# Cross-attention on one core: each group's output store sent as two DMAs divided at a partition that changes from group to group

## The chip, the cores and the metric

The kernel runs on one core of a Trainium2 chip. The core has five engines with queues of their own: TensorE (PE, with weight loads listed as PEld), VectorE (DVE), ScalarE (ACT), GpSimd (POOL) and SyncE (SP), which here only issues DMAs. 16 DMA engines move data between device memory and the on-chip memory of 128 partitions. The metric is the device time of one execution in microseconds. The kernel before took 1207.94 us in the median of 3 runs (1204.18 to 1209.92).

## The reference, cut to what matters

```
B, H, Sq, Sk, D = 16, 32, 192, 1024, 128          # bf16 inputs q, k, v
scores = einsum("bhqd,bhkd->bhqk", q, k) * D ** -0.5
p = softmax(scores, axis=-1)
out = einsum("bhqk,bhkd->bhqd", p, v)
```

There are 512 heads, each with 192 rows of queries and 1024 keys. The output has 98,304 rows of 128 bf16 values, 256 bytes each.

## The kernel before, in words

The 512 heads are worked through in 32 groups of 16 (G=16, L34). Two heads form a pair with 384 query rows, which are three units of 128 rows: the first 128 rows of one head (A), the last 128 of the other (B), and one made of the 64 rows left over from each (S). A group has 8 pairs and 24 units.

Each unit passes through five steps: TensorE multiplies Q by K into PSUM (qk, L237 to L270); VectorE copies the scaled scores out and takes the row maximum (rowmax, L328 to L335); the exponential is taken by ScalarE directly (L373), or, for the units named in SHIFTED, GpSimd subtracts the maximum (L207) and ScalarE takes the exponential later (L384); TensorE transposes the result in 8 blocks (tr, L272 to L283) and ScalarE moves it out of PSUM (L384, L386); TensorE multiplies it by V (pv, L285 to L319). VectorE then normalises a pair with one multiplication into the tile ob (outputs, L347 to L362). The order of the steps on TensorE, VectorE and ScalarE is written out by hand in PE_ORDER, DVE_ORDER and ACT_ORDER (L17 to L20), with a period of six units.

All DMAs are issued by SyncE, in the order of its program (L136 to L193). K, Q and V have two buffers each (NS=2), the output tile ob has two as well (NSO=2, slot so = g % 2). For each group g SyncE does this:

- `loads(g + 2)` (L157 to L165): waits on s_qk until TensorE has done the last Q-K product of group g, which frees the buffers of K and Q; issues the transposing load of K (L141, 4 MB) and that of q (L145, 768 KB); waits on s_pv until group g's last product with V is done; issues the load of V (L152, 4 MB, 2 KB runs).
- `stores(g, ...)` (L167 to L174): waits on s_on until VectorE has written all 8 pairs of group g, and issues the store of 768 KB (L170). Its source is 128 partitions with 24 rows of 256 bytes each.

So the DMAs stand in the queue as K, q, V, store, K, q, V, store, one set for each group. The first group's loads are cut into three pieces (FIRST), the last group's store into four (LAST): 31 stores of 768 KB and one each of 384, 192, 96 and 96 KB, 35 in all.

A DMA adds 16 to its semaphore when it has landed, one for each of 16 completions. `store_cnt(g)` (L127) gives the count of sst at which group g's store is done; VectorE waits for it before the first pair of group g+2 overwrites the slot (L352, L353), and SyncE waits at the end for all stores (L189 to L193). TensorE waits for K and q of a group in qk (L256 to L268) and for V in pv (L306 to L313).

Of the kernel before, what the change touches and what calls it, by code (L numbers as in the profile page):

```python
# [31 lines left out]


def _attention_kernel(nc, q, k, v, out, G=16, NS=2, NSS=4, NX=4, NPT=5,  # L34
                      FIRST=((0, 2), (2, 8), (8, 16)), LAST=((0, 4), (4, 6), (6, 7), (7, 8))):
    B, H, SQ, D = q.shape
    SK = k.shape[2]
    assert D == 128 and SK == 1024 and SQ == 192, (D, SK, SQ)
# [9 lines left out]
    NSO = 2  # L48
# [5 lines left out]
    of = out.rearrange("b h s d -> (b h) s d")  # L54
# [15 lines left out]
    with ExitStack() as es:  # L70
        def sb(name, shape, dt):
            return es.enter_context(nc.sbuf_tensor(name, shape, dt))
# [4 lines left out]
        def sem(name):  # L77
            return es.enter_context(nc.semaphore(name))
# [4 lines left out]
        ob = sb("ob", [128, NSO, PPG, 3, 128], BF16)  # L83
# [14 lines left out]
        svl = [sem("svl%d" % i) for i in range(NS)]  # L98
        sf = [sem("sf%d" % i) for i in range(len(FIRST))]
        sfv = [sem("sfv%d" % i) for i in range(len(FIRST))]  # L100
        sst = [sem("sst%d" % i) for i in range(NSO)]
# [23 lines left out]
            return 16 * (g // NS + 1 - (g % NS == 0))  # L125

        def store_cnt(g):  # L127
            return 16 * (g // NSO + 1)

        def wait_x(eng, u):  # L130
            eng.wait_ge(s_xp if shifted(u) else s_xa, x_cnt[u])  # L131
# [4 lines left out]
        @block.sync  # L136
        def _(e):
            def load_kq(g, a, b, sems):
                s = g % NS
                h0 = g * G  # L140
                e.dma_start_transpose(  # L141
                    kt[:, s, :, a * 128:b * 128],
                    kf[h0 + a:h0 + b].rearrange("g (p t) d -> (g p) (t d)", t=KT_TILES),
                ).then_inc(sems[0], 16)
                e.dma_start_transpose(  # L145
                    qt[:, s, a * SQ:b * SQ],
                    qf[h0 + a:h0 + b].rearrange("g r d -> (g r) d"),
                ).then_inc(sems[1], 16)

            def load_v(g, a, b, sm):  # L150
                h0 = g * G
                e.dma_start(  # L152
                    vs[:, g % NS, a:b],
                    vf[h0 + a:h0 + b].rearrange("g (p t) d -> p g t d", t=KT_TILES),
                ).then_inc(sm, 16)

            def loads(g):  # L157
                s = g % NS
                last_u = (g - NS + 1) * UPG - 1
                if g >= NS:  # L160
                    e.wait_ge(s_qk, last_u + 1)
                load_kq(g, 0, G, (sxk[s], sxq[s]))
                if g >= NS:
                    e.wait_ge(s_pv, last_u + 1)
                load_v(g, 0, G, svl[s])  # L165

            def stores(g, a, b):  # L167
                so = g % NSO
                e.wait_ge(s_on, g * PPG + b)
                e.dma_start(  # L170
                    of[g * G + 2 * a:g * G + 2 * b].rearrange("h r d -> (h r) d").rearrange(
                        "(n p) d -> p n d", p=128),
                    ob[:, so, a:b].rearrange("p pg y d -> p (pg y) d"),
                ).then_inc(sst[so], 16)  # L174

            n = len(FIRST)
            for i in range(n):
                load_kq(0, *FIRST[i], (sf[i], sf[i]))
                if i > 0:
                    for i2 in range(i if i > 1 else 0, i + 1):  # L180
                        load_v(0, *FIRST[i2], sfv[i2])
            for g in range(1, min(NS, NGR)):
                loads(g)
            for g in range(NGR):
                if g + NS < NGR:
                    loads(g + NS)
                for a, b in (LAST if g == NGR - 1 else ((0, PPG),)):
                    stores(g, a, b)
            for so in range(min(NSO, NGR)):  # L189
                n_uses = len(range(so, NGR, NSO))  # L190
                if so == (NGR - 1) % NSO:
                    n_uses += len(LAST) - 1
                e.wait_ge(sst[so], 16 * n_uses)  # L193

        @block.gpsimd
        def _(gp):
# [20 lines left out]
        def _(pe):  # L217
# [19 lines left out]
            def qk(u):  # L237
# [13 lines left out]
                if g == 0:  # L251
                    for i, (h, _) in enumerate(FIRST):
                        if h <= b and i not in seen_kq:
                            seen_kq.add(i)
                            pe.wait_ge(sf[i], 32)
                elif u % UPG == 0:  # L256
                    pe.wait_ge(sxq[s], load_cnt(g))
# [27 lines left out]
            def pv(u):  # L285
# [14 lines left out]
                for t in range(KT_TILES):  # L300
                    first = t == 0
                    last = t == KT_TILES - 1
                    for at, rows, x in tiles:
                        w = PTS[:, t, rows]
                        pe.ldweights(w, tile_position=at)  # L305
                        if first and at[1] == 0:  # L306
                            if g == 0:
                                for i, (h, _) in enumerate(FIRST):
                                    if h <= b and i not in seen_v:
                                        seen_v.add(i)  # L310
                                        pe.wait_ge(sfv[i], 16)
                            elif u % UPG == 0:
                                pe.wait_ge(svl[s], load_cnt(g))  # L313
                            if k3 == 0 and pr >= 2:
                                pe.wait_ge(s_on, pr - 1)
                        ins = product(O[rows, sl, :], w, vs[:, s, x, t, :], at, first, last)
                        if with_rs:
                            ins = product(O[rows, 3, sl: sl + 1], w, ones[:, 0:1], at, False, last)
# [8 lines left out]
        def _(dve):  # L327
# [19 lines left out]
            def outputs(pr):  # L347
                g = pr // PPG
                pg = pr % PPG
                so = g % NSO  # L350
                dve.wait_ge(s_pv, max(pv_cnt[u] for u in pair_units(pr)))
                if pg == 0 and g >= NSO:  # L352
                    dve.wait_ge(sst[so], store_cnt(g - NSO))  # L353
                sel = slots_of(pr, True)
                dve.reciprocal(rinv[:, pr % 2, sel], o_ps[pr % 2][:, 3, sel]).then_inc(s_ri, 1)  # L355
                dve.wait_ge(s_ri, 2 * pr + 2)
                dve.tensor_tensor(  # L357
                    ob[:, so, pg],
                    o_ps[pr % 2][:, 0:3, :],
                    rinv[:, pr % 2, 0:3].unsqueeze(2).to_broadcast([128, 3, 128]),  # L360
                    ALU.mult,
                ).then_inc(s_on, 1)  # L362
# [30 lines left out]
def bass_standalone__mha_softmax__near_ridge_kernel(  # L393
    nc: bass.Bass,
    q: bass.AP,
    k: bass.AP,
    v: bass.AP,
    out: bass.AP,
):
    _attention_kernel(nc, q, k, v, out)  # L400
# [28 lines left out]
```

## Time and profile before

| | before |
|---|---|
| median of 3 runs | 1207.94 us (1204.18 to 1209.92) |
| profiled execution | 1203.52 us, of which the span is 1201.8 us |
| busy: PE, PEld, DVE, ACT, POOL | 94%, 70%, 91%, 90%, 40% |
| DMA | 321.34 MB, mean 267 GB/s; 789,893 packets, of them 724,176 under 512 B |
| issue to landing, median: K, q, V, store of 768 KB | 30.4, 6.1, 15.1, 17.1 us |
| chain that ended last | PE 51%, DMA 34%, SP's queue 14% of the span |
| DVE wait for PE s_ps, ACT wait for PE pt_ps (L386) | 77.1 us, 78.4 us |

The span is the time from the first to the last instruction of the profiled execution. A busy share is an average over the whole span. DMA rates of the profile count all 16 engines together, so that one engine that moves 256-byte packets alone shows as a small number in a window of short slices. In lists of instructions, "SPq" stands for SyncE's queue: its time is the time for which an issuing instruction was held, not the time of the transfer. A line such as "L220 PE MATMUL o_ps<-vs,pt_sb" names the helper `product`, which records every product; the tiles tell which step it is.

### The profile page before, as it was taken

The page shows a single profiled execution, that of the slowest core. Times are in us where ns is not written, and L with a number is a line of the kernel's source. Part 1 is how long each engine was busy: PE and PEld are TensorE (multiplying, and loading weights), DVE is VectorE, ACT ScalarE, POOL GpSimd, SP SyncE. Part 2 cuts the span into 40 slices and gives each one's busy share as a digit, 9 for nine tenths or more (in the row PEclk, how much of TensorE's full clock was granted, in tenths as well). Part 3 has the DMA queues.
Part 4 walks back from the last instruction along what each step waited for, and adds up shares of the span by engine and source line. Part 5 has one row for each costly group of instructions (what it writes and reads, how often), then busy time and mean ns, then how long its engine had stood idle before and what let it go on. Part 6 is the DMA issues. An engine that isn't in the chain of part 4 may idle for free.

```text
span 1201.8 us, 40191 instructions
## 1 busy us (share of the span) xinstructions
PE 1123.8 (94%) x18432; PEld 844.7 (70%) x15360; DVE 1089.6 (91%) x2304; ACT 1083.3 (90%) x1793; POOL 485.3 (40%) x262
## 2 busy tenths in 40 slices
PE   5599999999999999999999999999999899999998
PEld 3477777777677777776776777777776667777776
DVE  5589998999899999999998999999998899989897
ACT  4689998999899999999998999999998899989898
POOL 2234443444343443443434444343443344334343
PEclk9899999999999999999999999999999999999999
DMA  9999999999999999999999999999999999999991
GB/s 238 238 280 293 264 279 263 267 295 265 289 269 254 275 294 289 274 279 251 279 289 268 293 259 259 295 278 288 291 230 264 281 284 288 264 248 295 275 274 41
DMA packets 789893, 321.34 MB, mean 267 GB/s; under 512 B 724176, under 2 KB 724176, under 8 KB 789712
## 3 DMA queue, kind: packets, MB, share of 16 engines
q1 hardware_dynamic: 789712, 318.78, 111.9%
q8 instruction: 132, 2.16, 0.7%
q14 instruction: 49, 0.40, 0.1%
HBM read 134.22 MB, written 25.17 MB: 133 GB/s over the span
## 4 chain that ended last, share of the span: by engine, by line
PE 51%; DMA 34%; SPq 14%; issue 1%; ACT 1%; DVE 0%; DVEq 0%
DMA vs<-in_v_dram 34%; PE o_ps L220 18%; PE pt_ps L220 17%; PE s_ps L220 16%; SPq L145 8%; SPq L141 5%; ACT x_sb L373 0%; DVE ss L332 0%; SPq L152 0%; ACT pt_sb L384 0%; ACT pt_sb L386 0%; DVE ob L357 0%; DVE rinv L355 0%; DVEq L131 0%
## 5 line engine op out<-in xcount | busy, mean ns | idle before, releaser
L332 DVE TENSOR_SCALAR_CACHE_REDUCE ss<-s_ps 128x1024 f32<-128x1024 f32 x768 | 920.8, 1220 | 95.8 <-PE s_ps L220 77.1
L207 POOL TENSOR_TENSOR x_sb<-ss,nb 128x1024 bf16<-128x1024 f32 x256 | 484.6, 1893 | 704.5 <-DVE ss L332 689.0
L305 PEld LDWEIGHTS <-pt_sb 128*128 128x128 bf16 (+1 forms) x8192 | 442.0, 104 | 238.0 <-issue 140.4
L373 ACT ACTIVATE x_sb<-ss,nb 128x1024 bf16<-128x1024 f32 x512 | 585.4, 1145 | 12.7 <-DVE ss L332 12.7
L220 PE MATMUL o_ps<-vs,pt_sb 128*128 128x128 bf16 (+1 forms) x8192 | 495.9, 219 | 38.6 <-DMA vs<-in_v_dram 38.5
L220 PE MATMUL s_ps<-kt,qt 128*128 128x512 bf16 (+1 forms) x2048 | 466.2, 386 | 35.0 <-DMA qt<-in_q_dram 33.5
L220 PE MATMUL pt_ps<-ident,x_sb 128*128 128x128 bf16 x6144 | 451.3, 220 | 1.3 <-ACT pt_sb L384 1.3
L279 PEld LDWEIGHTS <-x_sb 128*128 128x128 bf16 x6144 | 366.2, 98 | 62.5 <-issue 62.1
L386 ACT ACTIVATE pt_sb<-pt_ps 128x512 f32<-128x512 f32 x512 | 306.0, 598 | 78.6 <-PE pt_ps L220 78.4
L384 ACT ACTIVATE pt_sb<-pt_ps 128x1024 bf16<-128x1024 bf16 x256 | 260.1, 1016 | 21.9 <-PE pt_ps L220 21.9
L220 PE MATMUL o_ps<-ones,pt_sb 128*128 128x1 bf16 x2048 | 189.3, 165 | 0.0
L357 DVE TENSOR_TENSOR ob<-o_ps,rinv 128x384 bf16<-128x384 f32 x256 | 142.7, 557 | 8.8
L263 PEld LDWEIGHTS <-qt 128*128 128x128 bf16 (+1 forms) x1024 | 79.3, 103 | 53.3 <-DMA qt<-in_q_dram 30.5
L373 ACT ACTIVATION_READ_ACCUMULATOR x_sb<-ss,nb 128x1 f32 x512 | 100.7, 197 | 0.0
L332 DVE DVE_READ_ACCUMULATOR ss<-s_ps 128x1 f32 x768 | 63.7, 83 | 0.0
L355 DVE RECIPROCAL rinv<-o_ps 128x1 f32<-128x1 f32 x256 | 41.7, 163 | 4.3 <-PE o_ps L220 4.3
L345 DVE RECIPROCAL rinv<-rs 128x2 f32<-128x2 f32 x256 | 40.9, 160 | 1.1 <-ACT x_sb L373 1.1
L373 ACT ACT_TABLE_LOAD x1 | 1.3, 1283 | 0.8 <-PEq L414 0.8
L199 POOL TENSOR_SCALAR_AFFINE_SELECT ident<-ones 128x128 bf16<-128x128 bf16 x1 | 0.3, 292 | 0.1
L197 POOL MEMSET ones<- 128x128 bf16 x1 | 0.2, 204 | 0.3 <-POOLq L414 0.3
L414 POOL MEMSET const-float32-0.0<- 128x1 f32 x1 | 0.1, 98 | 0.3 <-issue 0.3
L414 POOL MEMSET const-bfloat16-1.0<- 128x1 bf16 x1 | 0.1, 101 | 0.0
(2 smaller groups left out, 0.2 us busy)
## 6 DMA issues: line engine op xcount, KB each, us to landing
vs<-in_v_dram SPq DMA_DIRECT2D x31, 4096.0 KB, 15.1
out_dram<-ob SPq DMA_DIRECT2D x31, 768.0 KB, 17.1
vs<-in_v_dram SPq DMA_DIRECT2D x1, 2048.0 KB, 10.4
vs<-in_v_dram SPq DMA_DIRECT2D x1, 1536.0 KB, 8.4
kt<-in_k_dram SPq DMA_TRANSPOSE x34, 30.4
qt<-in_q_dram SPq DMA_TRANSPOSE x34, 6.1
vs<-in_v_dram SPq DMA_DIRECT2D x1, 512.0 KB, 4.4
out_dram<-ob SPq DMA_DIRECT2D x1, 384.0 KB, 3.2
```

The source lines that it names most:

```text
L141: e.dma_start_transpose(kt[:, s, :, a * 128:b * 128], kf[h0 + a:h0 + b].rearrange("g (p t) d -> (g p) (t d)", t=KT_TILES),).then_inc(sems[ ...
L145: e.dma_start_transpose(qt[:, s, a * SQ:b * SQ], qf[h0 + a:h0 + b].rearrange("g r d -> (g r) d"),).then_inc(sems[1], 16)
L207: gp.tensor_tensor(x_sb[:, u % NX, :], ss[:, u % NSS, :], nb[:, u % NSS: u % NSS + 1].to_broadcast([128, SK]), ALU.subtract,).then_inc(s_x ...
L220: return pe.add_instruction(mybir.InstMatmult(name=nc.get_next_instruction_name(), engine=mybir.EngineType.PE, ins=[pe.lower_ap(x), pe.low ...
L263: pe.ldweights(w, tile_position=at)
L279: pe.ldweights(w, is_transpose=True, tile_position=(0, 0))
L305: pe.ldweights(w, tile_position=at)
L332: dve.tensor_scalar(ss[:, u % NSS, :], s_ps[u % 2][:].rearrange("p t k -> p (t k)"), -scale, None, ALU.mult, ALU.min, accum_out=nb[:, u % ...
L357: dve.tensor_tensor(ob[:, so, pg], o_ps[pr % 2][:, 0:3, :], rinv[:, pr % 2, 0:3].unsqueeze(2).to_broadcast([128, 3, 128]), ALU.mult,).then ...
L373: act.activation(x_sb[:, u % NX, :], ss[:, u % NSS, :], ACT_FN.Exp, bias=nb[:, u % NSS: u % NSS + 1], scale=-1.0, accum_out=rs[:, pr % NRS ...
L384: act.activation(pt_sb[:, u % NPT], pt_ps[u % 2][:], ACT_FN.Exp, scale=-1.0).then_inc(s_ev, 1)
L386: act.activation(words(pt_sb[:, u % NPT]), words(pt_ps[u % 2][:]), ACT_FN.Copy).then_inc(s_ev, 1)
```

## The change

Each store is issued as two DMAs. The first carries partitions 0 to cut-1, the second the rest. The cut is 126 for group 0, 117 for group 1, 108 for group 2, 121 for group 3, and so on in turn. Both DMAs add 16 to the same semaphore, so the counts that are waited for are doubled. The four pieces of the last group (group 31) are each divided at 121. The order in SyncE's queue, all waits of the other engines and the bytes moved stay the same.

```diff
 def _attention_kernel(nc, q, k, v, out, G=16, NS=2, NSS=4, NX=4, NPT=5,
-                      FIRST=((0, 2), (2, 8), (8, 16)), LAST=((0, 4), (4, 6), (6, 7), (7, 8))):
+                      FIRST=((0, 2), (2, 8), (8, 16)), LAST=((0, 4), (4, 6), (6, 7), (7, 8)), STORE_CUTS=(126, 117, 108, 121)):
...
         def store_cnt(g):
-            return 16 * (g // NSO + 1)
+            return 32 * (g // NSO + 1)
...
             def stores(g, a, b):
                 so = g % NSO
                 e.wait_ge(s_on, g * PPG + b)
-                e.dma_start(
-                    of[g * G + 2 * a:g * G + 2 * b].rearrange("h r d -> (h r) d").rearrange(
-                        "(n p) d -> p n d", p=128),
-                    ob[:, so, a:b].rearrange("p pg y d -> p (pg y) d"),
-                ).then_inc(sst[so], 16)
+                rows = of[g * G + 2 * a:g * G + 2 * b].rearrange("h r d -> (h r) d").rearrange(
+                    "(n p) d -> p n d", p=128)
+                cut = STORE_CUTS[g % len(STORE_CUTS)]
+                for lo, hi in ((0, cut), (cut, 128)):
+                    e.dma_start(
+                        rows[lo:hi],
+                        ob[lo:hi, so, a:b].rearrange("p pg y d -> p (pg y) d"),
+                    ).then_inc(sst[so], 16)
...
-                e.wait_ge(sst[so], 16 * n_uses)
+                e.wait_ge(sst[so], 32 * n_uses)
```

## The prediction

> **What bounds the kernel now.** I read the page's busy rows first, then the waits, then the sync queue's timeline, then the DMA rates in short windows.
>
> ```profile
> PE 1123.8 (94%) x18432; PEld 844.7 (70%) x15360; DVE 1089.6 (91%) x2304; ACT 1083.3 (90%) x1793; POOL 485.3 (40%) x262
> ...
> DMA  9999999999999999999999999999999999999991
> ...
> L220 PE MATMUL o_ps<-vs,pt_sb 128*128 128x128 bf16 (+1 forms) x8192 | 495.9, 219 | 38.6 <-DMA vs<-in_v_dram 38.5
> ```
>
> TensorE, VectorE and ScalarE are each busy 90% or more, yet TensorE still waits 38.5 us for V, 27 times, about once in each group of 16 heads, and the DMA row is full to the end. So the pace comes from the DMA engines, with TensorE close behind. From 400 to 1000 us TensorE waits 24.3 us for V in some 16.5 groups, 1.5 us in each. A group takes 36.4 us from V's arrival to the next V's arrival (mean over the trace's 31 V completions), so with no wait TensorE could do it in about 34.9: no gain here can pass 1.5 us a group.
>
> The sync queue in one period:
>
> ```profile
> 493.63 0.58 SPq L152 DMA_DIRECT2D vs<-in_v_dram  x1
> 494.25 4.52 SPq L170 DMA_DIRECT2D out_dram<-ob  x1
> 498.82 26.36 SPq L141 DMA_TRANSPOSE kt<-in_k_dram  x1
> 525.22 4.49 SPq L145 DMA_TRANSPOSE qt<-in_q_dram  x1
> 529.75 0.58 SPq L152 DMA_DIRECT2D vs<-in_v_dram  x1
> ```
>
> The four kinds of DMA follow one another without a gap: V, store, K transpose, q transpose. The view of waits puts 790 us of L141 down to TensorE's s_qk, but K's packets are flowing during that "wait"; the instruction is held because the queue in front of it is full. What the engines do at the seam from store to K transpose, in slices of 0.2 us from 504 to 512:
>
> ```profile
> DMA  9999999999999999999999999997321238999999
> GB/s 369 389 399 369 399 379 369 399 348 389 399 389 392 320 311 369 276 283 274 278 279 283 284 288 289 287 254 174 85 49 36 64 92 200 238 172 247 283 292 291
> ```
>
> V runs at 370 to 400 GB/s until 507, the store at about 280 until 509.2. Then the rate falls to 36 GB/s: most of the 16 engines have finished their share, and two have not. The transposes reach their full 290 GB/s only at 511.4. The trace records 16 completions for each store; here 14 of them come from 509.52 to 510.24 and two at 511.33 and 511.36. Over the 29 stores in front of a K transpose, the 14th of 16 comes on the average 0.86 us after the first, the 15th 1.47 and the last 1.96. In the trace the full rate starts within 0.4 us of that last completion in nearly all of the 29. **So a store costs the path what its latest engine costs**; the others wait for it.
>
> Why do the transposes wait for one engine? A window inside a K transpose, 0.1 us a slice from 481 to 485, shows it:
>
> ```profile
> GB/s 292 289 294 287 287 289 443 274 269 271 205 20 18 3 0 0 0 3 8 8 10 10 8 10 10 118 289 289 287 294 297 289 287 287 289 289 294 289 289 289
> ```
>
> At 481.6 one 16 KB packet of queue q8 (TensorE's instruction fetch: 132 packets, 2.16 MB) goes in. All transposing stops for 1.5 us, during which a lone engine catches up at 8 to 10 GB/s, and then all go on. The transposes move in step, so one late engine stops all 16. The late engines of a store are likewise those that a fetch has hit during V or the store: fetches come every 8.8 us and take 1.04 us.
>
> **The change, part by part.** It alters only SP's list: 35 store DMAs become 70, and every other instruction keeps its place. No instruction of another engine moves; only their line numbers do.
>
> 1. *How the load is dealt.* Now 128 partitions x 24 rows of 256 B = 3072 packets, 192 for each of 16 engines, 8 partitions each. No DMA of this trace has another number of partitions than 128, so the dealing of 126 is my assumption: equal whole shares, on as many engines, at most 16, as divide the number, from the first engine on. Then 126+2 gives 14 engines 9 partitions and two of these one more; 117+11 gives 10 on eleven engines, 9 on two; 108+20 gives 11 on ten, 9 on two; 121+7 gives 12 on seven, 11 on four. Heaviest engine against 8 partitions: +48, +48, +72 and +96 packets. At 290 GB/s / 16 a packet takes 14.1 ns, so +0.68, +0.68, +1.02, +1.36 us. Two to five engines, the last in number, get nothing: 2.7 us less.
> [...]
>
> 2. *Which engines are late now.* This decides the sign. The one place where I can count them is the tail, where DMAs start on idle engines. The store of 192 KB around 1193.3, in slices of 0.1 us from 1193 to 1197:
>
> ```profile
> GB/s 0 0 0 54 230 243 220 218 210 212 210 359 108 8 0 0 0 0 0 0 0 3 8 8 10 8 10 10 3 0 0 0 0 0 0 0 0 0 0 0
> ```
>
> A fetch goes in at 1194.16, and one engine does the second half of its share alone, from 1195.1. In the three other stores of the tail the 16 engines end in a staggered order, about 11 ns apart with a step after the seventh. Laid on that order, the 15 undisturbed ends miss the last but one: shifted by 8 to 16 ns all others fit, and with any other place left out the fit is worse. If engines are started in the order of their numbers, the fetch sits on the 15th, which gets no store at all after the change. That is one fetch; that the second late engine is its neighbour is a guess. I take both as relieved.
>
> 3. *The sum.* With the two late engines empty, a store ends with its 14 others, 0.86 us after the first, plus what these got. The latest of them is not always among the heaviest: I take 1.25 us (126), 1.5 (117), 1.8 (108), 2.05 (121), between "latest engine is heaviest" (1.54, 1.54, 1.88, 2.22) and a median engine at 0.3 (0.98, 0.98, 1.32, 1.66). The 29 stores are 8, 7, 7, 7: (8x1.25 + 7x1.5 + 7x1.8 + 7x2.05)/29 = 1.64 against 1.96: **-0.32 us each, -9.3 us**. The ends are -0.18 (-5 us) and -0.74 (-21 us).
>
> 4. *Lead into the transposes.* An engine that ends early does some 600/14 = 40 packets of K (0.6 us) before it must wait (counted in the trace's packets before the full rate). A relieved engine keeps this lead when a fetch hits it in K. Bounds: 0 and 29 x 0.6 = -17 us. I take 0, since the other engines have the same lead today; the end is kept for the range.
>
> 5. *SP's issue.* A store's issue now takes 4.5 us, V's 0.58: it is held by full queues, and the shortest store issue is 0.37 us (tail). Heaviest queues need 48 to 96 more places, which V clears at 11.4 us/128 = 89 ns each: the issue ends 4.3 to 8.5 us later, at 503 to 507.3, behind which stands only the K transpose, needed from 509.9 on. Cost nothing; the cover is the rest of V and the store. Were it gone, each us would be one per group, 29 us. The second issue (0.37 to 0.58 us) lies inside that time.
>
> 6. *The waits.* The counts double with the completions, so they mean the same. VectorE's wait for the store of two groups ago passes now 2.8 us early (landed 511.36, used at 514.18) and stays early by 1.4 us at +1.36.
>
> 7. *Tail.* The last store (24 packets an engine) has 36 on the heaviest: 12 x 18 ns = 0.2 us, and a second issue at 0.37: +0.6 us.
>
> Sum: -9.3 + 0.6 = -8.7 us. The profiled execution took 1203.52 us (span 1201.8 and 1.7 around it), so 1194.8; the median of the three runs, 1207.94, lies 4.4 higher, and the same difference gives **1199 us**.
>
> **The rivals.** *A late engine that carries more (slower).* If fetches hit engines that keep their store, every store ends later. On the heaviest: 15 x 0.68 + 7 x 1.02 + 7 x 1.36 = +26.9 us, 1235. If the late place wanders over all 16, weighting each engine's end gives +0.28, +0.44, +0.67, +0.96, together 16.7 us, 1225. It decides as soon as the heaviest late engine ends after 1.96 us. For it: the heaviest load rises under all four cuts, and in 20 of 29 stores two late engines must both be relieved. Against: the tail's fetch.
>
> *One relieved, one not.* In the 20 stores with more late ends the second, at 1.47 plus a mean of 0.84, ends at 2.31 (+0.35 each, +7); the other nine gain 0.32: about +4, 1212.
>
> *Nothing moves.* If both DMAs are spread over all 16 engines, loads stay 8 partitions each, and only the tail pays: 1208.5. For it: the equal dealing is all the trace has.
> [...]
>
> **How the numbers follow.** 0.5%, 6 us, is about what a measurement can tell from no change. Forecast 0.50, of which 0.44 lies beyond -6 us; slower rival 0.22; one relieved 0.15 (0.06 slower, 0.09 same); nothing moves 0.13 (0.01 either side, 0.11 same). Faster 0.45, same 0.26, slower 0.29. The forecast's own range is 1180 to 1204: part 3's far end with some of part 4's lead below. To hold 8 in 10 the range must reach into the slower rival's nearer form: 1180 to 1228, leaving out its 1235 form and the deepest lead.
>
> **What would show it.** Right: at the seam the slices at 36 to 85 GB/s shrink or vanish, completions of a store no longer have one or two 1 us behind, TensorE's wait for V falls by some 9 us, and K transposes start 0.3 us earlier after V. Wrong: that tail of the seam grows by 0.7 to 1.4 us and the wait for V by 17 to 27 us. Stalls inside K shorter than 1.5 us would show part 4. A K transpose that begins late with idle engines would show part 5 wrong.

## The result, and the profile after

| | before | after |
|---|---|---|
| median | 1208.18 us (4 runs, 1204.18 to 1209.92) | 1221.17 us (4 runs, 1218.88 to 1221.73) |
| ratio after / before | 1 | 1.0109, interval 1.008 to 1.0137 |
| profiled execution, span | 1203.52, 1201.8 us | 1221.69, 1220.0 us |
| V's last completion to the next V's last, mean over 29 stores | 36.55 us | 37.22 us |
| from V's first completion to the store's last | 4.50 us | 5.05 us |
| from V's first completion to the K transpose's last | 22.38 us | 23.04 us |

The change makes the kernel slower by 1.1%, 13.0 us. The forecast was 1199 us. The last three rows are means over the 29 stores that stand in front of a K transpose, taken from the completions in the trace. Such a mean of the store's end has a standard error of about 0.1 us over the 29 stores (0.06 before, 0.12 after). A period grew by 0.67 us; 29 of them are 19.4 us, and the two spans differ by 18.2. The profiled execution of before is shorter than all four of its runs, so the spans lie further apart than the medians. Of the 0.67 us, 0.55 are there when the store ends.

From the page of after: busy times, the DMA row and packet counts, and the two groups of products that wait for loads (busy, mean ns of one, then idle time and what ended it).

```profile
PE 1126.4 (92%) x18432; PEld 846.5 (69%) x15360; DVE 1090.2 (89%) x2304; ACT 1085.6 (89%) x1793; POOL 485.8 (40%) x262
...
DMA  9999999999999999999999999999999999999991
...
DMA packets 790027, 321.34 MB, mean 263 GB/s; under 512 B 724310, under 2 KB 724310, under 8 KB 789846
...
L223 PE MATMUL o_ps<-vs,pt_sb 128*128 128x128 bf16 (+1 forms) x8192 | 496.6, 219 | 38.3 <-DMA vs<-in_v_dram 38.2
L223 PE MATMUL s_ps<-kt,qt 128*128 128x512 bf16 (+1 forms) x2048 | 466.7, 386 | 50.5 <-DMA qt<-in_q_dram 50.0
```

The engines do the same work (TensorE +2.6 us), the bytes are the same, and the DMA row is still full. What grew is TensorE's wait for loads: for q from 33.5 to 50.0 us, for V not at all (38.5 to 38.2). The line of before for q:

```profile
L220 PE MATMUL s_ps<-kt,qt 128*128 128x512 bf16 (+1 forms) x2048 | 466.2, 386 | 35.0 <-DMA qt<-in_q_dram 33.5
```

These 16.5 us and the 2.6 together are about the 18.2 us of the spans. q is the load behind K, and K is the one behind the store. So the late seam shows first at the product that needs the K and q of the next group.

SyncE's queue in one period of after (start, time held, instruction):

```profile
496.19 4.76 SPq L145 DMA_TRANSPOSE qt<-in_q_dram  x1
501.00 0.59 SPq L152 DMA_DIRECT2D vs<-in_v_dram  x1
501.64 14.53 SPq L174 DMA_DIRECT2D out_dram<-ob  x2
516.23 16.60 SPq L141 DMA_TRANSPOSE kt<-in_k_dram  x1
```

The two issues of this store hold SyncE for 14.5 us where the one issue took 4.5. They end at 516.17, which is 1.9 us after V's first completion at 514.29. The K transpose has that much less time to be queued. The seam of this store, cut at 121, in slices of 0.2 us from 513 to 521:

```profile
DMA  9999998988888888888888898999399999999999
GB/s 399 379 410 351 321 376 207 219 204 198 202 197 198 197 204 198 202 197 198 197 204 198 200 209 200 238 239 175 40 152 285 288 288 291 293 291 289 289 288 291
```

From 514.2 to 518 the store runs at 198 GB/s where it ran at 280 before. That is 11 engines of 18 GB/s each: five engines stand still, 11 carry 11 partitions each and need longer. No engine is late here, and the transposes are at full rate from 519. Another store, cut at 108, from 473.6 to 481.6 (V's first completion at 476.46):

```profile
GB/s 410 440 369 389 379 369 399 379 399 389 369 374 343 306 247 307 198 214 202 196 207 207 210 216 218 216 215 169 128 143 143 136 132 127 95 150 150 206 154 228
```

Here a second stage of 128 to 143 GB/s follows the first, from 479.2 to 480.4: the partitions from 108 on. By the end of the window the transposes are not yet at full rate.

### The profile page after: what moved, and what is told of

The parts are those of the page before. It is cut to its first block, busy times and chain, and to the rows that moved or that the text cites. A ratio compares the mean times of both kernels' runs of the same rounds, so it can differ in the third digit from the quotient of the medians.

```text
span 1220.0 us, 40226 instructions
## 1 busy us (share of the span) xinstructions
PE 1126.4 (92%) x18432; PEld 846.5 (69%) x15360; DVE 1090.2 (89%) x2304; ACT 1085.6 (89%) x1793; POOL 485.8 (40%) x262
## 4 chain that ended last, share of the span: by engine, by line
PE 52%; DMA 35%; SPq 11%; ACT 1%; issue 1%; DVE 0%; DVEq 0%
DMA vs<-in_v_dram 32%; PE o_ps L223 19%; PE pt_ps L223 17%; PE s_ps L223 16%; SPq L145 6%; SPq L141 5%; DMA qt<-in_q_dram 3%; ACT x_sb L376 0%; DVE ss L335 0%; SPq L152 0%; ACT pt_sb L387 0%; ACT pt_sb L389 0%; DVE ob L360 0%; DVE rinv L358 0%; DVEq L131 0%
## 5 line engine op out<-in xcount | busy, mean ns | idle before, releaser
L223 PE MATMUL o_ps<-vs,pt_sb 128*128 128x128 bf16 (+1 forms) x8192 | 496.6, 219 | 38.3 <-DMA vs<-in_v_dram 38.2
```

What stands on the lines that cost most here:

```text
L223: return pe.add_instruction(mybir.InstMatmult(name=nc.get_next_instruction_name(), engine=mybir.EngineType.PE, ins=[pe.lower_ap(x), pe.low ...
```

## The experiments

Theories, by letter. **L**: the engines that end a store late still carry a share of it, so a store ends later as shares get heavier. **H** is the form of L in which the late place wanders over all engines, with the seam (the stretch between V and K's full rate) priced in packets of 14.1 ns: the rival at 1225. **S**: any second DMA adds a late stage of its own, whatever the shares. **P**: a DMA of few neighbouring partitions is slow whatever the shares, a guess of the author's. **B**: a small second DMA enters the queues when most engines have run dry.

"Store's end" is the mean time from V's first completion to the store's last, "period" that from V's last completion to the next V's last, both over 29 stores of the profiled execution. Each ratio is taken against runs of the kernel before that were made beside it; its median was 1205.70, 1206.65 or 1202.58 us there.

### A part of the store alone

Only the first 126, 104, 108 or 63 partitions are stored, in one DMA. The rest isn't stored.

```diff
-                        "(n p) d -> p n d", p=128),
-                    ob[:, so, a:b].rearrange("p pg y d -> p (pg y) d"),
+                        "(n p) d -> p n d", p=128)[0:126],
+                    ob[0:126, so, a:b].rearrange("p pg y d -> p (pg y) d"),
```

Expected of 126 (14 engines with 9 partitions each, if the dealing is right):

> The kernel before, but each store carries only partitions 0 to 125, in one DMA; the last two partitions of the tile are not stored. Theory of the prediction (the late engines are the last two, and get nothing): a store ends about 3.75 us after V's first completion instead of 4.50, some 22 us less in all, 1186 us. Theory L (the late engines are among those that keep a share, 9 partitions instead of 8): 4.84 us, 10 us more, 1218. Theory S (what costs is the second DMA, not the shares): as the prediction, 1186 or, if the late engines keep their share too, no more than 1218.

Expected of 104 (13 engines with 8 each; the last three engines empty and no share heavier than before):

> The kernel before, but each store carries only partitions 0 to 103, in one DMA; 24 partitions are not stored. If dealt in equal shares it is 8 partitions on 13 engines and nothing on three. Late engines among the last three: a store ends near 3.4 us instead of 4.50, 32 us less, 1176. Late engines elsewhere (theory L): every loaded engine has what it had, so 4.50 us and 1208, the same as before.

Expected of 108 (12 engines with 9 each):

> The kernel before, but each store carries only partitions 0 to 107, in one DMA; 20 are not stored. Dealt in equal shares it is 9 partitions on 12 engines. Theory H (what costs is the share of the late engine, whose place wanders over the 16): like the single DMA of 126, 0.2 us a store, 6 us, 1213. Theory B (what costs is the second DMA, which enters the queues when most engines have run dry) says the same or less.

Expected of 63 (9 engines with 7 each):

> The kernel before, but each store carries only partitions 0 to 62; the other 65 are not stored. Dealt in equal shares it is 7 partitions on 9 engines. With 13 engines the two late completions stayed, so the late engines are among the first 13. If they are among the first nine, the last completions still come one by one behind the others, near 3.9 us after V's first; if they are the tenth to thirteenth, the last comes near 2.9.

| stored alone | ratio to before | store's end, us | period, us | completions of a store | late ones in a store | stores with none late, of 29 |
|---|---|---|---|---|---|---|
| all 128 (before) | 1 | 4.50 | 36.55 | 16 | 1.83 | 0 |
| 126 | 1.0049 (1.0028 to 1.0069) | 4.71 | 36.74 | 14 | 1.66 | 2 |
| 108 | 0.9977 (0.9961 to 0.9992) | 4.49 | 36.57 | 12 | 1.17 | 8 |
| 104 | 0.992 (0.9895 to 0.9946) | 4.26 | 36.35 | 13 | 1.38 | 5 |
| 63 | one run: 1163.74 us beside 1206.65 | 3.34 | 35.20 | 9 | 0.62 | 20 |

"Late" is a completion over 0.85 us behind the median of its store. Two things follow.

The number of engines is as assumed: the completions count them. A DMA on fewer than 16 engines shows one event more, which comes about when its issue ends (0.17 us after it, the median over 58 issues of after) and isn't counted in the table. The changed kernel's stores show 18, 26, 24 and 20 events in turn: 14+2, 13+11, 12+10 and 11+7 completions, and one event more for each of the two DMAs. Each of the four counts, 14, 13, 12 and 9, is the largest divisor up to 16 of its 126, 104, 108 and 63 partitions. Which engines they are is not seen in the counts, so that the dealing begins at the first engine stays an assumption, and with it that a second DMA falls on engines which carry the first.

The late place wanders. A fixed late engine would be late in every store that uses it, yet with 63 partitions nine stores have late completions and 20 have none. If the last two engines had been the late ones, 104 partitions would have no late completions. The store would then end at the mean 14th completion of before, 3.40 us, 1.1 us earlier, 32 us in all. It ends 0.24 us earlier, 7 us in all, and the measured gain is 8.4 us (1205.7 to 1197.3). Late completions fall about with the number of engines that carry the store: 1.83 x 14/16 = 1.60 (found 1.66), x 13/16 = 1.49 (1.38), x 12/16 = 1.37 (1.17), x 9/16 = 1.03 (0.62). The last two fall further. So the late ones are neither the last engines alone nor the first nine alone.

The late completions also go with the instruction fetches (queue q8), as the prediction said. In the trace of before, 14 of the 29 stores have two fetches between 11.2 us before and 2.2 us after V's first completion, and all 14 have two or more late completions. The other 15 have one fetch, and all ten stores with a single late completion are among them. The place does not move at random either. With 63 partitions the nine stores with late completions are those of groups 4, 6, 8 and so on to 20, every second one without a gap. With 104, four of the five stores with none are those of groups 20, 22, 24 and 26. What rule this follows is not shown; it means that the 29 stores of one execution are not a chance sample.

A seam of the kernel that stores 104 partitions, from 504.1 (V's first completion at 507.11), has its late engine still:

```profile
GB/s 379 410 358 399 399 379 358 389 338 379 389 389 410 338 298 326 233 219 230 221 229 225 230 233 236 238 205 152 82 36 54 193 237 168 56 120 275 227 282 291
```

After the store's plateau at 230 GB/s (13 engines) the rate falls to 36, as before. Two seams of the kernel with 63 partitions, from 488.8 and from 382.8 (V's first completion at 491.83 and 385.79), show a store with no late engine and one with two:

```profile
GB/s 389 338 389 389 389 379 410 358 369 369 399 389 389 291 320 191 183 197 182 196 182 173 163 166 193 213 257 186 95 41 178 291 291 292 292 288 288 291 291 292
```

```profile
GB/s 389 410 410 399 410 389 410 389 399 379 399 369 330 333 219 188 168 189 161 175 157 163 163 164 106 51 37 118 46 140 184 173 152 33 47 14 9 36 285 288
```

In the first the transposes reach 291 GB/s at 495.0, 3.2 us after V. In the second they do so at 390.4, 4.6 us after V, with the rate down to 9 GB/s in between. Neither form of the expectation fits the mean of 3.34 us, as both had one fixed place.

A heavier share costs time. From 104 to 108 partitions each share in use grows by 24 packets (0.34 us) on one engine fewer, and the store ends 0.23 us later; the ratio goes from 0.992 to 0.9977. With 126 partitions each share has 24 packets more than before as well, and the store ends 0.21 us later. Against before, 108 costs nothing: the heavier share and the fewer late engines (1.17 for 1.83) about cancel.

### The second DMA, with one cut for all groups

```diff
-                      LAST=((0, 4), (4, 6), (6, 7), (7, 8)), STORE_CUTS=(126, 117, 108, 121)):
+                      LAST=((0, 4), (4, 6), (6, 7), (7, 8)), STORE_CUTS=(126,)):
```

Cut at 126, where the second DMA, as assumed, puts one partition more on two engines:

> The changed kernel with all stores cut at 126. Its own groups with this cut end a store 4.68 us after V's first completion, 0.18 later than before: 5 us more, 1213. Theory L says 0.34 later, 10 us, 1218; the prediction said 0.7 earlier, 1187.

Cut at 108, where, as assumed, it puts two more on ten engines:

> The changed kernel with all stores cut at 108. In its own groups with this cut a store ends 1.23 us later than before: 36 us, 1243. Theory H alone, 264 packets instead of 192 on ten engines, late place wandering: 0.67 us a store, 19 us, 1226.

Cut at 112, where 16 engines have 7 partitions and then one more each, 8 as before:

> The changed kernel with all stores cut at 112: 7 and 1 partitions on each of 16 engines, so no engine carries more than before. Theory S (the second DMA enters the queues late, behind the slowest engine's share of the first, and is a second small stage): a store ends 0.2 to 0.5 us later, 6 to 15 us more, about 1218. Theory L, and the prediction's price for the shares alone: only the tail's 0.6 us, 1208.5.

| cut | ratio to before | store's end, us | period, us | against the same first DMA alone |
|---|---|---|---|---|
| 126 | 1.0036 (1.0021 to 1.005) | 4.83 | 36.87 | 1211.53 against 1212.17 us |
| 108 | 1.0127 (1.0109 to 1.0145) | 5.10 | 37.10 | 1216.92 against 1200.54 us |
| 112 | 1.0166 (1.0135 to 1.0197) | 4.89 | 37.29 | not run |

At 126 the second DMA costs nothing that can be told (1211.53 us with it, 1212.17 without), although, as assumed, it puts one partition more on two engines. At 108, where by the same assumption it makes the share 48 packets heavier on ten of 12 engines, 0.68 us, the store ends 0.61 us later than with the first DMA alone. That is 29 x 0.61 = 17.7 us, and 16.4 were measured. For 108 theory H had 0.67 us a store and 19 us over before; found were 0.60 and 1.27%, 15 us. The 36 us taken from the changed kernel's own groups are a miss. So H fits both cuts. Cut 112 is a miss for H: the shares are even, and it is the slowest of all. Its seam from 512.4 (V's first completion at 515.37):

```profile
GB/s 399 369 399 379 389 420 358 379 410 369 379 399 396 265 284 275 283 284 282 283 283 278 289 291 225 91 45 36 86 115 108 108 101 146 170 164 197 116 26 69
```

The first DMA runs at about 283 GB/s to its end, the rate falls to 36, and only then do the second one's packets flow, at 108 GB/s. One store has two ends.

### Even shares, divided in three ways

`rows21` divides by rows: both DMAs span 128 partitions, with 21 and 3 of the 24 rows, 168 and 24 packets for each engine. `halves64` cuts at 64, and `evenodd` takes the even and then the odd partitions.

```diff
-                cut = STORE_CUTS[g % len(STORE_CUTS)]
-                for lo, hi in ((0, cut), (cut, 128)):
+                n = 3 * (b - a)
+                cut = n * 7 // 8
+                for lo, hi in ((0, cut), (cut, n)):
                     e.dma_start(
-                        rows[lo:hi],
-                        ob[lo:hi, so, a:b].rearrange("p pg y d -> p (pg y) d"),
+                        rows[:, lo:hi],
+                        ob[:, so, a:b].rearrange("p pg y d -> p (pg y) d")[:, lo:hi],
```

```diff
-                for lo, hi in ((0, cut), (cut, 128)):
+                for lo in (0, 1):
...
-                        rows[lo:hi],
-                        ob[lo:hi, so, a:b].rearrange("p pg y d -> p (pg y) d"),
+                        rows[lo:128:2],
+                        ob[lo:128:2, so, a:b].rearrange("p pg y d -> p (pg y) d"),
```

> The changed kernel, but each store is divided by rows, not by partitions: the first DMA has 21 of the 24 rows of all 128 partitions, the second the other 3. Packets per DMA and per engine are those of the cut at 112 (168 and 24). [...] Theory S (any second DMA comes late and costs a stage): as the cut at 112, 0.7 us a store, 1227.

> The changed kernel with all stores cut at 64. [...] Theory S: as the cut at 112, 1227.

> The changed kernel, but one DMA has the even partitions and the other the odd ones, 64 each as in the cut at 64. [...] Theory S: as the cut at 64 and at 112, 1227 or more.

| | ratio to before | store's end, us | period, us | SyncE held by both issues (one store), us | second issue ends, against V's first completion (the same store) |
|---|---|---|---|---|---|
| rows21 | 1.0115 (1.0098 to 1.0132) | 4.70 | 37.03 | 14.77 | 2.2 us after |
| cut 112 (above) | 1.0166 (1.0135 to 1.0197) | 4.89 | 37.29 | 14.87 | 2.2 us after |
| halves64 | 1.0015 (1.0 to 1.003) | 4.69 | 36.76 | 11.98 | 0.65 us before |
| evenodd | 1.0014 (0.9998 to 1.0031) | 4.56 | 36.53 | 11.32 | 1.3 us before |

In the mean over the 29 stores the second issue ends 2.1 us after V's first completion in rows21 and in cut 112, and 0.7 us before it in the other two.

Two equal halves cost nothing that can be told. So S falls as a rule for every second DMA. Nor is there a loss by P for halves of 64 neighbouring partitions: halves64 has them and evenodd spreads them, and their ratios are 1.0015 and 1.0014. A small second DMA costs 1.15% even with even shares over all partitions. B would have it so, for the small one enters late. But the store's end does not show it: 4.70 us in rows21 and 4.69 in halves64, which costs nothing (its profiled execution is 2.9 us above its median). B is open here. SyncE's queue in rows21, then in halves64:

```profile
499.22 0.58 SPq L152 DMA_DIRECT2D vs<-in_v_dram  x1
499.85 14.77 SPq L175 DMA_DIRECT2D out_dram<-ob  x2
514.68 16.37 SPq L141 DMA_TRANSPOSE kt<-in_k_dram  x1
```

```profile
496.29 0.59 SPq L152 DMA_DIRECT2D vs<-in_v_dram  x1
496.92 11.98 SPq L174 DMA_DIRECT2D out_dram<-ob  x2
508.96 18.73 SPq L141 DMA_TRANSPOSE kt<-in_k_dram  x1
```

V's first completion is at 512.41 in rows21 and at 509.55 in halves64. In rows21 the second DMA is in the queues at 514.62, when the first is all but done; in halves64 at 508.90, before the first has begun. Their seams, from 509.4 and from 506.6:

```profile
GB/s 399 399 369 399 389 379 420 348 379 379 348 379 399 374 306 310 372 280 275 284 273 282 280 279 275 260 154 59 87 244 201 60 37 110 150 189 223 236 229 72
```

```profile
GB/s 420 348 389 430 348 379 420 348 389 399 379 401 344 314 385 289 274 279 282 271 292 273 284 287 292 282 213 105 70 67 37 152 159 141 230 111 250 289 294 289
```

rows21 falls to 59 GB/s at 514.8, rises to 244 for the second DMA, and falls to 37 once more. halves64 falls once. What P says is seen in one place: with the same 24 packets for each engine, the second DMA of cut 112 (16 neighbouring partitions) flows at 108 GB/s, that of rows21 (all 128) at 244. Their stores end 0.19 us apart, 5.5 us in all, and their ratios differ by 0.5%, 6 us. Why 16 neighbouring partitions flowed at less than half that rate, no run shows. The plateau of halves64, whose first half is 64 neighbouring partitions, is at 271 to 292 GB/s from its start, so no loss of that kind shows there.

Of rows21's 0.48 us for a period, 0.20 are there at the store's end. The other 0.28 lie between it and K's end (18.17 us against 17.89; 17.91 in halves64; each with a standard error of 0.12 to 0.15). K's lead is shorter, 571 packets before the store's last completion against 657 before, but 86 packets are some 0.08 us at 290 GB/s (86 x 256 B). The rest is not explained.

### The order of the two DMAs

If a small second DMA that comes late were the main cause in the changed kernel, sending the small one first should win the loss back.

```diff
-                for lo, hi in ((0, cut), (cut, 128)):
+                for lo, hi in ((cut, 128), (0, cut)):
```

> The same cut, 108, but the DMA of 20 partitions is issued first and that of 108 second. The shares are those of the cut at 108, so theory H gives the same time for both. Theory B: the second DMA is now long and enters the queues while all engines are still busy with V, so what the cut at 108 loses by its small second DMA is won back: 0.5 us a store, 15 us less than the cut at 108, about 1226.

> The changed kernel with its four cuts, the small DMA of each store issued first. Theory H: as the changed kernel, 1221. Theory B: its part of the loss goes, some 0.2 us a store or 6 us, 1215; the shares keep the rest.

| | ratio to before | store's end, us | period, us |
|---|---|---|---|
| cut 108, small one second | 1.0127 (1.0109 to 1.0145) | 5.10 | 37.10 |
| swap108, small one first | 1.0099 (1.0084 to 1.0114) | 4.95 | 36.94 |
| the changed kernel | 1.0109 (1.008 to 1.0137) | 5.05 | 37.22 |
| swapall, four cuts, small ones first | 1.0102 (1.0084 to 1.012) | 4.99 | 36.94 |

In swap108 SyncE is free after 8.85 us where cut 108 held it for 14.39:

```profile
500.81 0.59 SPq L152 DMA_DIRECT2D vs<-in_v_dram  x1
501.45 8.85 SPq L174 DMA_DIRECT2D out_dram<-ob  x2
510.36 22.65 SPq L141 DMA_TRANSPOSE kt<-in_k_dram  x1
```

The K transpose's issue begins 8.9 us after the store's first issue and not 14.4 us after it, and the loss is nearly all still there. The intervals of swap108 and cut 108 touch (0.28% apart in the middle), those of swapall and the changed kernel cover each other. Theory B forecast 15 us less for swap108, and 0.28%, 3.4 us, was found. It forecast 6 us less for swapall, and 0.07%, 1 us, was found. So in the changed kernel neither the order nor SyncE's hold costs more than a small part.

P is a rival here too: at 108 the small DMA has 20 neighbouring partitions, and the seam from 473.6 above has them at 128 to 143 GB/s. The seam of swap108 from 510.6 (V's first completion at 513.91), where they go first:

```profile
GB/s 389 399 389 379 410 358 399 369 369 410 379 369 399 389 362 339 297 255 224 221 229 219 220 282 197 201 198 205 209 211 211 219 193 143 76 41 37 124 188 177
```

There is no slow stage of their own: the store runs at about 200 to 220 GB/s, 12 engines of 18, up to its late engines. In the mean over 29 stores, cut 108 stands at 124 to 156 GB/s from 2.8 to 4.6 us after V's first completion, and swap108 keeps to 200 or more until 3.2. So the slow second stage goes with the order, and 0.15 us of the store's end with it (5.10 to 4.95). The other 0.45 us over before stay. The heavier shares remain, which the order leaves as they are; H gave them 0.67. No run has these shares without a second DMA, so that they are the whole of the rest is argued.

## Why the prediction was wrong

**What bounds the kernel: right.** The DMA engines set the pace, and a store costs what its latest engine costs. The two kernels whose store ends clearly earlier than 4.50 us (63 and 104 partitions, 3.34 and 4.26 us) are faster, and most in which it ends clearly later are slower. The store's end is not all of it: rows21 and halves64 end theirs at 4.70 and 4.69 us, and only rows21 is slower.

**Step 1, the dealing: right as far as it is seen.** The counts of completions show the number of engines. No run shows that they are the first in number, nor that the second DMA's engines are among the first DMA's, from which the heaviest shares of 48 to 96 packets more were worked out. A packet costs what was assumed: 11 engines at 198 GB/s are 18.0 each, and 256 B at that rate take 14.2 ns.

**Step 2, which engines are late: the step that failed.** It read one fetch in the tail, put it on the 15th engine of 16, and said "I take both as relieved". The store of 104 partitions shows that emptying three engines, the last ones by the assumed dealing, wins 8.4 us and not 32, with 1.38 late completions in a store where none were to be left. One fetch told of one moment. The trace had 132 such packets, and the late place changes from store to store. So the late engines mostly kept their share, and the share had grown.

**Step 3, the sum.** Forecast -0.32 us for a store, found +0.55 (4.50 to 5.05). The wandering form of the first rival gave 16.7 us for all stores; 29 x 0.55 is 16.0, and the rival's 1225 us stands beside the measured 1221. Its sizes by cut were +0.28, +0.44, +0.67 and +0.96 for 126, 117, 108 and 121; found were +0.18, +0.57, +1.23 and +0.28. With 7 or 8 stores for each cut these tell little: in the kernel with one cut at 108, the same four sets of groups give 4.76 to 5.51 us with nothing to set them apart. The mean is what the rival got right, in part by luck: it had shares alone in its sum, and the second stage at 108 is not in it.

**Step 4, a lead into the transposes: right at nothing.** K's packets ahead of the store's last completion are 647 in after and 657 in before.

**Step 5, SyncE's issue: a wrong size with little effect.** It said that the issue ends 4.3 to 8.5 us later than 498.8, before V lands. The two issues hold SyncE for 14.5 us, 10 us longer than before, and end 1.9 us after V's first completion. From the store's end to K's end takes 17.99 us against 17.89, so about 0.1 us for a period goes there, 3 us in all, which is within the error.

**Steps 6 and 7.** The waits of after, like those of before, list none of VectorE for a store that has not landed. The tail's 0.6 us is too small to be told apart.

**The rivals.** "Nothing moves" fell with the dealing, "one relieved" with step 2. What was to show the slower rival was a longer seam and a wait for V larger by 17 to 27 us. The seam is longer, but the wait that grew is that for q, by 16.5 us.

Not settled: which engine each fetch hits is not seen, only how late completions come. How much of the loss at each cut is shares and how much the second stage that shows at 479.2, is told only for 108, where swapping the order wins back 0.28% of 1.27%. Why a small second DMA with even shares costs 1.15% is open.

## What to carry to other kernels

When a step can only go on once the slowest DMA engine is done, count what the heaviest engine gets. A split that gave some engines more and others nothing lost 1.1% here, because the late ones were not always the emptied ones (with three engines empty, 104 partitions, 1.38 late completions in a store stayed). To learn which ones those are, count late completions over all instances, or empty some engines and see; a single stall has one place and says nothing of the next. If a transfer must be divided, two equal parts with even shares cost 0.15% here (1.0015, interval 1.0 to 1.003), and a small remainder sent last, 3 rows of 24, cost more (1.0115).

## What the hardware did that was not expected

- **A small second DMA behind a large one made a gap of its own.** With even shares and all partitions, 21 rows and then 3 cost 1.15%; two equal halves by partitions cost 0.15%. The gap (59 GB/s at 514.8) is seen; that it is what costs is not shown.
- **The second issue of a store seems to be held until the slowest engine has some 120 to 145 packets left.** This is an estimate from when the issues end, in the mean over 29 stores. In rows21 that is 0.34 us after V's last completion: some 24 of the first DMA's 168 packets can be gone at 14.1 ns, and 144 are left. In halves64 it is 2.53 us before V's last completion: 28 packets of V at the prediction's 89 ns and the 96 of the first half are left, 124. No run varied it by itself.
- **16 neighbouring partitions flowed at 108 GB/s, all 128 at 244, with the same packets for each engine** (one seam each, cut 112 and rows21).
- **Fewer engines, fewer late ends.** With 9 of 16 engines in use, in one execution, 20 of 29 stores had none, and a V-to-V period took 35.20 us, near the 34.9 that TensorE's work alone was put at.
